# Turning a prologue block as even and odd rows in two column halves of the array, with a PSUM pair for the turns

## The chip, the cores and the metric

The kernel runs on one core of one Trainium2 chip. The metric is device time in microseconds of one execution, as the median of several runs. TensorE is called PE here (its weight loads PEld), VectorE DVE, ScalarE ACT, GpSimd POOL and SyncE SP. PE writes to PSUM, which has eight banks of 512 fp32 numbers in each of 128 partitions; ACT and DVE carry results from there to SBUF.

## The reference

Four sequences of 12544 positions and 128 channels go through a long convolution, and the result goes through a maxout feed-forward layer:

```python
h_filt = (np.maximum(pos_emb @ w1, 0.0) @ w2) * np.exp(-0.01 * pos)[:, None]
u = x * v
L = 2 * S
y = np.fft.irfft(np.fft.rfft(u, n=L, axis=1) * np.fft.rfft(h_filt, n=L, axis=0)[None], n=L, axis=1)[:, :S, :]
x = (x * y).reshape(B * S, D)                       # B=4, S=12544, D=128
h = np.maximum(np.maximum(x @ w1m, x @ w2m), x @ w3m)   # D -> 768
return h @ w_out                                    # 768 -> D
```

All of it is fp32, and the weights of the feed-forward layer come in as 64-bit numbers that the kernel converts.

## The kernel before, in words

A sequence's 12544 positions are 98 rows (`NB`) of 128. The Fourier transform is done as matrix products in two steps: a first one over the 98 rows with a table of 90 frequencies (`N1`), and a second one over the 128 positions of a row with twiddled tables. Batches 1 to 3 go through the transform beside the feed-forward layer of the batch before; batch 0 and the filter have a prologue of their own, which is what the change touches.

The schedule is written by hand: the program's order is each engine's order, and a tile framework adds the semaphores.

In the prologue the 128 channels of batch 0 are taken as 32 units (`u`) of 4 channels. For each unit, SP loads a block of `xr` and one of `vr` ([128, 4, 98], `u_load`, L381), DVE multiplies them in place (`u_mul`, L388), and PE turns the block so that the 98 rows come to lie on the partitions. `turn2(u)` (L987) turns two units at once: per unit four `nc.tensor.transpose` calls (L393), each with 98 columns of weights and the identity as the moving operand. The result is a PSUM pair (two banks, 1024 numbers in 98 partitions), which ACT copies to the tile `uT` (L993). `uT` has two buffers.

The first step is `quad` (L996), which calls `first_halves` (L172): 16 times two matmuls, in the profile 32 a quad at L178. Each takes 64 columns of `uT` as weights and 90 columns of the table `f1` as the moving operand, and goes to one half of the array's columns (PSUM partitions 0 to 63 or 64 to 127). The contraction runs over the 98 partitions. One ACT copy (L187, 128 x 720) then empties the PSUM pair. Everywhere else in the kernel the pattern is the same: two matmuls side by side in the two column halves (`halves_mm`, L169).

PSUM is four pairs, `acc[0]` to `acc[3]`, all of one name in the profile (`ps`). `turns_` hands them out. In the filter's MLP (first 38 us) it cycles over `acc[0]` and `acc[1]`, while `mlp_in` (L355, tiles of 64 rows and 41 columns) and `mlp_out` (DVE) use `acc[2]` and `acc[3]`. Afterwards it cycles over all four, in the order 2, 3, 0, 1, and turns and quads draw from the same cycle. Rows 32 to 63 of `acc[2]` and `acc[3]` are set to zero at the start (L305).

The order on PE is: warm-up matmuls; the MLP with two turns (units 0 and 1, then 2 and 3) and four early quads in between; 16 quads of the filter with two turns among them; then for each pair of units two quads and the turn of the pair after next. Loads for a pair of units are issued when a turn has freed its block six units back. Beside it DVE converts weights in small steps (`some`). After the last quad the pools are closed and the second stage begins (L1110, L169, L1135 and so on), in which `u_turn` (L395, matmul at L401) already turns blocks as even and odd rows in two column halves: `a[:, i, p::2]`, 49 columns each, to PSUM partitions 0 to 48 and 64 to 112.

Of the kernel before, what the change touches and what calls it, by code (L numbers as in the profile page):

```python
# [10 lines left out]
FP32 = mybir.dt.float32  # L11
# [5 lines left out]
P = 128  # L17
# [8 lines left out]
N1 = 90  # L26
# [5 lines left out]
def e(t):  # L32
    return np.exp(2j * np.pi * (t - np.floor(t)))


def stacked(c):

    top = np.concatenate([c.real, c.imag], -1)
    bottom = np.concatenate([-c.imag, c.real], -1)
    return np.concatenate([top, bottom], -2)  # L40


def tables(NB):
    S = P * N1
    k1 = np.arange(N1).reshape(2, N1 // 2).T.ravel()
    n = np.arange(NB)
    a = e(np.outer(n, k1 + 0.25) / N1)
    f1 = np.concatenate([a.real, a.imag], 1)
    up = e(np.outer(n + 0.5, k1 + 0.25) / N1)
    f1e = np.zeros((64 + NB // 2, 2, N1))  # L50
    for p in range(2):
        for h, t in enumerate((up, a)):
            t = t[p::2, ::2]
            f1e[64 * p:64 * p + NB // 2, h] = np.concatenate([t.real, t.imag], 1)
    f1h = np.zeros((64 + HH, 2, 2 * N1))
    f1h[:HH, 0], f1h[64:, 0] = f1[:HH], f1[HH:NH]
    f1h[:HH, 1], f1h[64:, 1] = f1[HH:NH], f1[:HH]
    f4 = np.stack([a.T.real, a.T.imag], 1) / S
    f4p = f4[::2].transpose(1, 0, 2).reshape(N1, NB // 2, 2).transpose(0, 2, 1)
    f4 = np.stack([up.T.real, up.T.imag], 1) / S  # L60
    f4s = f4[::2].transpose(1, 0, 2).reshape(N1, NB // 2, 2).transpose(0, 2, 1)
    f4q = np.stack([f4p, f4s * np.array([1, -1])[:, None]], 1)
    j, t = np.arange(64), np.arange(64)
    tw = (k1[:, None, None] + 0.25) / S
    half = []
    for r in range(2):
        s2 = (127 - 2 * t - r)[None, :, None]
        half.append(stacked(e(tw * s2 + j[None, None, :] * s2 / 128)))
    fwd = np.stack(half, 2)
    half = []  # L70
    for q in range(2):
        s2 = (2 * t + q)[None, None, :]
        half.append(stacked(e(-tw * s2 - j[None, :, None] * s2 / 128)))
    inv = np.stack(half, 2)
    both = np.stack([fwd, inv], 2)
    both = both.reshape(N1 // 2, 2, P, 2, 256).transpose(0, 2, 3, 1, 4)
    both = both.reshape(N1 // 2, P, 2, 512)
    j, t = np.arange(32), np.arange(32)
    quarter = [[], []]
    for v in range(2):  # L80
        for w in range(2):
            s2 = (63 - 2 * t - v)[None, :, None]
            quarter[0].append(stacked(e(tw * s2 + (2 * j + w)[None, None, :] * s2 / 128)))
            s2 = (2 * t + w)[None, None, :]
            quarter[1].append(stacked(e(-tw * s2 - (2 * j + v)[None, :, None] * s2 / 128)))
    quarter = np.stack([np.stack(q, 1) for q in quarter], 1)
    quarter = quarter.reshape(N1 // 2, 2, 2, 2, 2, 64, 64).transpose(0, 3, 5, 2, 1, 4, 6)
    quarter = quarter.reshape(N1 // 2, P, 2, 256)
    steps = np.zeros((N1 // 2 + LATE, P, 2, 256))
    steps[:N1 // 2, :, 0], steps[LATE:, :, 1] = quarter[:, :, 0], quarter[:, :, 1]  # L90
    f32 = np.float32
    return tuple(np.ascontiguousarray(t, f32) for t in (f1, f1e, f1h, f4q, both, steps))


@with_exitstack
def kernel(
# [15 lines left out]
    nc = tc.nc  # L112
    NG, _, _, B, NB = x.shape
# [9 lines left out]
    const = ctx.enter_context(tc.tile_pool(name="const", bufs=1))  # L123
# [8 lines left out]
    ze = dram.tile([2, 2, 2, 256], FP32, name="ze")  # L132

    f1_t, f1e_t, f1h_t, f4p_t, w_t, wq_t = tables(NB)
    f1_d = nc.inline_tensor(f1_t, name="f1_const").ap()
    f1e_d = nc.inline_tensor(f1e_t, name="f1e_const").ap()
# [4 lines left out]
    HB = NB // 2  # L141
    HR = 64 + HB
# [6 lines left out]
    w_sb = [None] + [const.tile([D, DFF], FP32, name=f"w_sb{i}") for i in (1, 2)]  # L149
    wo_sb = const.tile([P, NF, D], FP32, name="wo_sb")  # L150
    lin = const.tile([D, D], FP32, name="lin")
    f1_sb = const.tile([NB, 2 * N1], FP32, name="f1")
    f1 = f1_sb[:]
    f1e = const.tile([64 + NB // 2, 2, N1], FP32, name="f1e")
    spec = const.tile([P, N1, 2, D], FP32, name="spec")
# [8 lines left out]
    def halves_mm(out, lhsT, rhs, start, stop):  # L164


        w = block[0]
        for h in range(0, P, w):
            nc.tensor.matmul(out[h:h + w], lhsT[:, h:h + w], rhs,  # L169
                             start=start, stop=stop, skip_group_check=True)  # L170
# [95 lines left out]
    utp = ctx.enter_context(tc.tile_pool(name="utp", bufs=2))  # L266
    pro = ExitStack()
    raw0 = pro.enter_context(tc.tile_pool(name="raw0", bufs=1))
    eye = raw0.tile([P, P], FP32, name="eye")
# [5 lines left out]
    sml = fin.enter_context(tc.tile_pool(name="sml", bufs=1))  # L275
    fps = fin.enter_context(tc.tile_pool(name="fps", bufs=1, space=PSUM))
    acc = [fps.tile([P, 1024], FP32, name=f"ps{i}") for i in range(4)]
    turns_ = itertools.cycle(acc[:2])

# [17 lines left out]
    f1h = sml.tile([64 + HH, 2, 2 * N1], FP32, name="f1h")  # L299
    warm = sml.tile([P, 256], FP32, name="warm")  # L300
    nc.vector.memset(warm[:], 0.0)
    nc.vector.memset(win, 0.0)
    pms = acc[2:]
    for pm in pms:
        nc.vector.memset(pm[32:64], 0.0)  # L305
    for h in range(2):
        nc.gpsimd.dma_start(
# [14 lines left out]

    def warm_up(n):

        ps = next(turns_)
        for _ in range(n):
            halves_mm(ps[:, 0:256], warm[:, 0:P], warm[:], True, True)

    pw = next(turns_)

    def window_turn():
        nc.tensor.transpose(pw[:, 0:64 + HH], win, eye[0:64 + HH, 0:64 + HH])
# [11 lines left out]
    def w2_order():  # L344
        nc.scalar.copy(w2x[:].rearrange("f (c g) -> f c g", c=GC),
                       w2_in[:].rearrange("f (g c) -> f c g", c=GC))
# [22 lines left out]
    us, uts, ws, hts, eos, xts, xss, abs_, pss, sqs, zss = ({} for _ in range(11))  # L369
# [16 lines left out]
    def u_mul(u, eng=nc.vector):  # L386
        a, v = us[u]
        eng.tensor_tensor(out=a[:], in0=a[:], in1=v[:], op=ALU.mult)  # L388

    def turn(u, ps):  # L390
        a, _ = us.pop(u)
        for i in range(4):
            nc.tensor.transpose(ps[0:NB, i * P:(i + 1) * P], a[:, i, :], eye[:])  # L393

    def u_turn(u):  # L395
        if u % 2 == 0:
# [589 lines left out]

    def turn2(u):  # L987

        t = utp.tile([NB, 8, 2, 64], FP32, tag="uT", name="uT")
        ps = next(turns_)  # L990
        for v in range(2):
            turn(u + v, ps[:, 512 * v:512 * v + 512])
        nc.scalar.copy(t[:], ps[0:NB, :].rearrange("n (s t r) -> n s r t", s=8, r=2))  # L993
        uts[u] = t

    def quad(lhs, table, *dsts, engines=(nc.scalar.copy, nc.scalar.copy)):  # L996
# [8 lines left out]
    def early(u):  # L1005
        t, v = uts[u - u % 2], 4 * (u % 2)
        quad([t[:, v + i] for i in range(4)], (f1, f1), aside[u],
             spec[:, NS:, :, 4 * u:4 * u + 4])

    warm_up(22)  # L1010
    window_turn()
    warm_up(3)
    nc.scalar.dma_start(f1, f1_d)
    for u in range(4):
# [5 lines left out]
    for i in range(9):  # L1020
        if i in (4, 7):
            turn2(2 * (i // 7))
            for u in range(6 + 2 * (i // 7), 8 + 2 * (i // 7)):
                u_load(0, u)
        if i in (5, 6):
            early(i - 5)
        if i < 8:
            mlp_in(i)
        if i >= 7:
            early(i - 5)  # L1030
        if i == 0:
            window_back()
            nc.scalar.dma_start(f1h[:], f1h_d)
            nc.scalar.dma_start(w2_in[0:FO], w2[:, :])
            nc.scalar.dma_start(w2_in[FO:P], w2[:, :])
        else:
            mlp_out(i - 1)
        if i in (3, 5):
            for u in range(i - 3, i - 1):
                u_mul(u)  # L1040
# [1 line left out]
    for u in (0, 2):  # L1042
        uts.pop(u)
    w2_order()
    turns_ = itertools.cycle(acc[2:] + acc[:2])
    for f in range(0, FO, 4):
        quad([hs[:, f + i] for i in range(4)], (f1h[:, 0], f1h[:, 1]), specH[:, :, :, f:f + 4])
        u, k = divmod(f // 4, 4)
        if u < 2:
            if k in (0, 1):  # L1050
                u_mul(2 * u + 4 + k)
            if k == 2:
                turn2(2 * u + 4)
                for v in range(2 * u + 10, 2 * u + 12):
                    u_load(0, v)
        some(2 if u < 2 and k < 2 else 3)
# [3 lines left out]
    for u in range(4, NU, 2):  # L1060
        t = uts.pop(u)
        for v in range(2):
            if u + 4 < NU:
                u_mul(u + 4 + v)
            at = 4 * (u + v)
            dst = spec[:, :, :, at:at + 4]
            quad([t[:, 4 * v + i] for i in range(4)], (f1, f1),
                 *([dst] if u + v < NU - 1 else [dst[:, :NK], dst[:, NK:]]),
                 engines=copies if u + v == NU - 1 else copies[:1])
            some(1)  # L1070
        if u + 4 < NU:
            turn2(u + 4)
        for v in (u + 10, u + 11):
            if v < NU:
                u_load(0, v)
        if u in (22, 24, 26):
            wf[(u - 22) // 2] = load_dir((u - 22) // 2, 0)
            wi[(u - 22) // 2] = load_dir((u - 22) // 2, 1)
        some(2)
# [261 lines left out]
    for i in range(0, NT, 2):  # L1341
        h = {}
        X, Y = banks if i % 4 == 0 else banks[::-1]
        for j, (name, f) in enumerate(ORDER):
            n = int(name[1]) - 1
# [66 lines left out]
```

## Time and profile before

| | us |
|---|---|
| median of three runs | 2207.23 (2205.39 to 2209.17) |
| the profiled execution | 2205.64 |
| its span | 2203.9 |
| PE busy | 2186.5 (99%) |
| turns of the prologue (L393) | 128 matmuls, 24.1 to 104 |
| prologue's last quad | ends at 109.3 |
| second stage's first matmul (L1110) | 110.41 |

The page's first lines give the busy time of each engine and its share of the span. A line of the order of time has a start, a length, the engine, the line of the kernel, the operation, the tiles written and read, the array's tile (rows by columns), the moving operand's shape and a count. The length of a group reaches to the end of its last matmul, which overlaps the next group; the pace is therefore read from start to start. A table of stretches has a row for each stretch with the busy time of each engine (with the number of instructions), PE's granted clock as a share of full speed, and the DMA's share and rate.

### The profile page before, as it was taken

To read this page: it belongs to the slowest core of one execution; us is meant where nothing else is said; L and a number is where in the kernel's file an instruction comes from. 1 tells how busy PE (TensorE), PEld (TensorE's weight loads), DVE (VectorE), ACT (ScalarE), POOL (GpSimd) and SP (SyncE) were. 2 spreads that over 40 slices of the span, in tenths; PEclk is the share of its full clock that TensorE was granted. 3 is DMA by queue.
4 is the path that set the end of the run, shared out by engine and by line. 5 is a ranking of instruction groups with operands and counts; after the bars stand their busy time and mean duration, and the time that the engine had idled before them with its cause. 6 is when DMAs were issued, how large, how long until landed. Compare 5 with 4: busy or idle time off the path is not lost.

```text
span 2203.9 us, 77207 instructions
## 1 busy us (share of the span) xinstructions
PE 2186.5 (99%) x31655; PEld 1258.5 (57%) x31655; DVE 1533.7 (70%) x3292; ACT 1211.4 (55%) x2223; POOL 1183.3 (54%) x1580
## 2 busy tenths in 40 slices
PE   9999999999999999999999999999999999999998
PEld 8988855555555555555555455555555545555565
DVE  5688966678888766668888766668878745454443
ACT  3699845466666555466666555456666522222222
POOL 1166568545544667535455566534545326666665
PEclk9999999999999999999999999999999999999999
DMA  8789999879999899789999899879999622222221
GB/s 200 184 262 318 302 181 206 170 196 247 248 245 246 209 189 178 155 193 243 245 245 251 212 193 175 171 172 244 242 251 241 179 75 59 65 71 69 59 59 24
DMA packets 491270, 411.62 MB, mean 187 GB/s; under 512 B 289379, under 2 KB 407901, under 8 KB 490917
## 3 DMA queue, kind: packets, MB, share of 16 engines
q1 hardware_dynamic: 443495, 274.33, 57.5%
q0 software_dynamic: 45936, 130.43, 20.9%
q8 instruction: 249, 4.08, 0.8%
q10 hardware_dynamic: 1486, 1.93, 0.4%
q14 instruction: 104, 0.85, 0.1%
HBM read 262.85 MB, written 84.68 MB: 158 GB/s over the span
## 4 chain that ended last, share of the span: by engine, by line
PE 93%; DVE 2%; POOL 2%; issue 1%; DMA 0%; ACT 0%; POOLq 0%; ACTq 0%; DVEq 0%
PE hps L169 46%; PE ops L169 20%; PE ops L913 6%; PE cps L169 4%; PE cps L549 3%; PE cps L451 3%; PE ps L178 3%; PE cps L559 3%; PE ps L169 2%; POOL xt L640 1%; PE last L169 1%; DVE ab L647 1%; PE ps L393 1%; DVE xs L639 1%; POOL specH L640 1%
## 5 line engine op out<-in xcount | busy, mean ns | idle before, releaser
L169 PE MATMUL hps<-gt,w_sb 128*64 128x392 f32 (+1 forms) x7672 | 1151.8, 494 | 1.8 <-DVE hid L852 1.0
L849 ACT ACTIVATE hid<-hps 128x392 f32<-128x392 f32 x768 | 382.4, 498 | 745.2 <-PE hps L169 726.9
L169 PEld LDWEIGHTS hps<-gt,w_sb 128*64 128x64 f32 (+1 forms) x7672 | 413.7, 126 | 454.5 <-issue 415.9
L852 DVE TENSOR_TENSOR hid<-hid,hps 128x392 f32<-128x392 f32 x768 | 428.5, 558 | 339.9 <-PE hps L169 321.4
L169 PE MATMUL ops<-hid,wo_sb 128*64 128x392 f32 x2304 | 476.8, 492 | 0.0
L601 POOL TENSOR_TENSOR cb<-cb,xs 128x512 f32<-128x512 f32 x135 | 178.2, 1320 | 358.3 <-DVE xs L598 349.8
L169 PEld LDWEIGHTS ops<-hid,wo_sb 128*64 128x64 f32 x2304 | 165.7, 137 | 213.5 <-issue 213.5
L574 DVE TENSOR_TENSOR cb<-cps,eo 128x512 f32<-128x512 f32 (+1 forms) x288 | 175.2, 650 | 78.0 <-ACT eo L571 76.9
L867 POOL DMA_DIRECT2D out_dram<-ot x96 | 77.1, 803 | 263.6 <-ACT ot L865 247.3
L589 ACT ACTIVATE xs<-cb 32x512 f32<-32x512 f32 x270 | 169.5, 628 | 21.9 <-DVE cb L574 13.1
L590 ACT COPY xs<-cb 32x512 f32<-32x512 f32 x270 | 166.3, 616 | 3.1
L605 DVE TENSOR_TENSOR xs<-cb 128x256 f32<-128x256 f32 x270 | 148.3, 598 | 7.3 <-POOL cb L601 7.3
L431 ACT COPY uT<-turned 113x512 uint16<-113x512 uint16 x180 | 125.9, 770 | 1.9 <-DMA turned<-planes 1.7
L388 POOL TENSOR_TENSOR ut<-ut 128x392 f32<-128x392 f32 x90 | 92.8, 1032 | 43.1 <-DMA ut<-in_vr_dram 42.9
L582 POOL DMA_DIRECT2D zd<-cb x135 | 93.8, 695 | 39.9 <-DVE cb L574 36.8
L169 PEld LDWEIGHTS cps<-f4p,even 90*64 90x64 f32 x1552 | 87.2, 138 | 35.9 <-issue 33.1
L777 POOL DMA_DIRECT2D xT<-in_x_dram x172 | 101.4, 605 | 4.6 <-DVE ab L647 3.1
L473 DVE TENSOR_TENSOR low<-high,cps 128x180 f32<-128x180 f32 x186 | 54.7, 336 | 68.9 <-ACT high L463 68.9
L938 POOL DMA_DIRECT2D out_dram<-o x120 | 72.6, 610 | 45.6 <-DVE o L931 44.5
L169 PE MATMUL cps<-f4p,zt 90*64 90x49 f32 x1552 | 95.9, 222 | 0.0
L415 POOL COPY planes<-ut 128x392 uint16<-128x392 uint16 x180 | 94.9, 561 | 0.0
L169 PE MATMUL cps<-f4p,even 90*64 90x49 f32 x1552 | 94.6, 220 | 0.0
(173 smaller groups left out, 3306.1 us busy)
## 6 DMA issues: line engine op xcount, KB each, us to landing
ht<-hd SPq DMA_DIRECT2D x264, 256.0 KB, 6.8
wt<-wq_const POOLq DMA_DIRECT2D x144, 256.0 KB, 5.6
zd<-cb POOLq DMA_DIRECT2D x135, 256.0 KB, 5.1
zt<-zd SPq DMA_DIRECT2D x384, 90.0 KB, 3.8
sq<-spec SPq DMA_DIRECT2D x528, 64.0 KB, 5.9
ut<-in_xr_dram SPq DMA_DIRECT2D x128, 196.0 KB, 4.0
ut<-in_vr_dram SPq DMA_DIRECT2D x128, 196.0 KB, 4.3
wt<-wt_const SPq DMA_DIRECT2D x90, 256.0 KB, 5.1
```

Source lines behind the costliest of these rows:

```text
L169: nc.tensor.matmul(out[h:h + w], lhsT[:, h:h + w], rhs, start=start, stop=stop, skip_group_check=True)
L415: nc.gpsimd.tensor_copy(w[:, h, :, :, 0:HB], a[:].bitcast(U16).rearrange("p s (m e h) -> p h s e m", e=2, h=2)[:, h])
L431: nc.scalar.copy(uts[u][0:HR, 8 * (u % 2):8 * (u % 2) + 8].rearrange("n s r t -> n (s r t)").bitcast(U16).rearrange("n (s r t h) -> n h s ...
L574: nc.vector.tensor_tensor(out=cb[:, a, lo:hi], in0=ps[:, lo:hi], in1=eo[:, lo:hi], op=op)
L589: nc.scalar.mul(xs[at:at + 32], xt[at + 32:at + 64], -1.0)
L590: nc.scalar.copy(xs[at + 32:at + 64], xt[at:at + 32])
L601: nc.gpsimd.tensor_tensor(out=xts[g], in0=xts[g], in1=xs[:], op=ALU.add)
L605: nc.vector.tensor_tensor(out=ab[:, q], in0=y[:, 0], in1=y[:, 1], op=(ALU.subtract, ALU.add)[q])
L777: eng.dma_start(xT[c * NG:(c + 1) * NG].rearrange("d i p n -> d (i p) n"), x[:, 4 * i:4 * i + 8, c, b, :])
L849: nc.scalar.activation(h[:], pa[:, 0:N], Relu)
L852: nc.vector.tensor_tensor(out=h[:], in0=h[:], in1=pb[:, 0:N], op=ALU.max)
L913: nc.tensor.matmul(ps[32 * q:32 * q + 32, 0:H2], w[:, m:m + 32], rhs[:, H2 * c:H2 * c + H2], start=start, stop=True, skip_group_check=True)
```

## The change

`turn2` no longer calls `turn` (which goes away) but multiplies the even rows and the odd rows of the block with the identity, as two matmuls of 49 columns in the two column halves. `uT` then has the even rows in partitions 0 to 48 and the odd ones in 64 to 112, and nothing in between. The table `f1` is laid out to match: `f1x` has 113 rows, with zeros in rows 49 to 63. The turns always use `acc[1]`, whose rows 32 to 63 are set to zero at the start. The quads use `acc[0]`, `acc[0]`, `acc[0]`, `acc[2]` in the MLP part and then cycle over `acc[0]`, `acc[3]`, `acc[2]`. The warm-up goes to `acc[0]`. Here `HB` is 49 and `HR` 113.

```diff
+    f1x = np.zeros((64 + NB // 2, 2 * N1))
+    f1x[:NB // 2], f1x[64:] = f1[::2], f1[1::2]
...
-    return tuple(np.ascontiguousarray(t, f32) for t in (f1, f1e, f1h, f4q, both, steps))
+    return tuple(np.ascontiguousarray(t, f32) for t in (f1x, f1e, f1h, f4q, both, steps))
...
-    f1_sb = const.tile([NB, 2 * N1], FP32, name="f1")
+    f1_sb = const.tile([HR, 2 * N1], FP32, name="f1")
...
-    turns_ = itertools.cycle(acc[:2])
+    turns_ = iter((acc[0], acc[0], acc[0], acc[2]))
...
-    for pm in pms:
+    for pm in acc[1:]:
         nc.vector.memset(pm[32:64], 0.0)
...
-        ps = next(turns_)
         for _ in range(n):
-            halves_mm(ps[:, 0:256], warm[:, 0:P], warm[:], True, True)
-
-    pw = next(turns_)
+            halves_mm(acc[0][:, 0:256], warm[:, 0:P], warm[:], True, True)
+
+    pw = acc[0]
...
-    def turn(u, ps):
-        a, _ = us.pop(u)
-        for i in range(4):
-            nc.tensor.transpose(ps[0:NB, i * P:(i + 1) * P], a[:, i, :], eye[:])
...
-        t = utp.tile([NB, 8, 2, 64], FP32, tag="uT", name="uT")
-        ps = next(turns_)
+        t = utp.tile([HR, 8, 2, 64], FP32, tag="uT", name="uT")
+        ps = acc[1]
         for v in range(2):
-            turn(u + v, ps[:, 512 * v:512 * v + 512])
-        nc.scalar.copy(t[:], ps[0:NB, :].rearrange("n (s t r) -> n s r t", s=8, r=2))
+            a, _ = us.pop(u + v)
+            for i in range(4):
+                for p in range(2):
+                    nc.tensor.matmul(
+                        ps[64 * p:64 * p + HB, 512 * v + i * P:512 * v + (i + 1) * P],
+                        a[:, i, p::2], eye[:], start=(i == 0), stop=True,
+                        skip_group_check=True)
+        nc.scalar.copy(t[:], ps[0:HR, :].rearrange("n (s t r) -> n s r t", s=8, r=2))
...
-    turns_ = itertools.cycle(acc[2:] + acc[:2])
+    turns_ = itertools.cycle((acc[0], acc[3], acc[2]))
```

## The prediction

> **What bounds the kernel now.** I read the page first (busy shares), then a table of busy time for the stretches of the prologue, then the PE's order of time in that stretch, and last the DVE's, to see what feeds the turns. The page:
>
> ```profile
> span 2203.9 us, 77207 instructions
> PE 2186.5 (99%) x31655; PEld 1258.5 (57%) x31655; DVE 1533.7 (70%) x3292; ACT 1211.4 (55%) x2223; POOL 1183.3 (54%) x1580
> ```
>
> The PE is busy for 99% of the span, so a microsecond of PE work taken out is a microsecond of time unless another engine then holds the PE up. The turns all lie between 24 and 104 us. One stretch of the table from one turn's start to the next, and one of the PE in order of time (start, length, line, names, count):
>
> ```profile
> core 0: us, PE busy (x) PEld busy (x) DVE busy (x) ACT busy (x) POOL busy (x), PEclk, DMA share, GB/s
> 66.68:70.32 3.64, 3.64 (x75) 3.35 (x73) 1.03 (x2) 2.53 (x3) 0.00 (x0) 1.00 1.18 296
> ...
> 88.52:92.17 3.65, 3.65 (x75) 3.36 (x73) 3.29 (x8) 2.54 (x3) 0.00 (x0) 1.00 0.92 218
> ```
>
> ```profile
> 31.27 1.87 PE L355 MATMUL ps<-w_sb,specH 64*41 64x64 f32 x64
> 33.06 1.08 PE L393 MATMUL ps<-eye,ut 128*98 128x128 f32 x8
> 34.08 1.75 PE L355 MATMUL ps<-w_sb,specH 64*41 64x64 f32 x64
> 35.75 2.70 PE L178 MATMUL ps<-f,uT 98*64 98x90 f32 x64
> ...
> 43.12 5.18 PE L178 MATMUL ps<-f1h,spec 105*64 105x90 f32 x128
> 48.23 1.08 PE L393 MATMUL ps<-eye,ut 128*98 128x128 f32 x8
> 49.24 11.38 PE L178 MATMUL ps<-f1h,spec 105*64 105x90 f32 x288
> 60.45 2.65 PE L178 MATMUL ps<-f,uT 98*64 98x90 f32 x64
> 63.04 1.08 PE L393 MATMUL ps<-eye,ut 128*98 128x128 f32 x8
> 64.05 2.70 PE L178 MATMUL ps<-f,uT 98*64 98x90 f32 x64
> 66.68 1.08 PE L393 MATMUL ps<-eye,ut 128*98 128x128 f32 x8
> ```
>
> The reader is to see that the PE never pauses here at full clock, that ACT has over a microsecond to spare in 3.64, and that a cycle is one turn (1.01 from its start to the next group's) and two quads (64 matmuls, 2.63). The same half-array turn that the change brings already runs later, in `u_turn`, again between other matmuls of the PE:
>
> ```profile
> 236.88 1.09 PE L169 MATMUL ps<-ab,wt 128*64 128x128 f32 x16
> 237.81 1.04 PE L401 MATMUL pst<-eye,ut 128*49 128x128 f32 x16
> 238.68 0.61 PE L1110 MATMUL gps<-wt,specH 128*64 128x128 f32 x8
> 239.12 1.04 PE L169 MATMUL ps<-spec,wt 128*64 128x128 f32 x16
> ```
>
> **The change part by part.** Sums are made against the profiled execution: 2205.64 us, of which 2203.9 is the span. It lies 1.59 under the median of the three runs (2207.23), and I add that back at the end.
>
> *Turns.* Removed: 8 full-array transposes per `turn2`, 1.01 us (64.05 - 63.04), so 127 ns each. Added: 16 matmuls of 49 columns by 128. L401 runs exactly this form, 16 in 0.87 us (238.68 - 237.81), 54.4 ns each. Saved 0.14 us. The 16 weight loads (8 before) take 124 ns each in both forms, but in L401 they lie under the other half's matmuls, or the pace couldn't be 54.4.
>
> *The bubble ahead of a turn.* From 43.12 to 48.23 are 128 quad matmuls and one change to a turn, 5.11 us; from 49.24 to 63.04 are 352 and one change, 13.80. The difference is 8.69 for 224, 38.8 ns each. 64 of them take 2.48, yet between turns they take 2.63: 0.15 us go each time the PE passes from halves to the full array. Around L401 I see none: 16 in 0.87 before L1110, which then runs 8 in 0.44, the same 54 ns. After the change turn and quad both use the full rows in two column halves, as L169 and L401 do. The cost of the new passage isn't in the trace: between nothing (L401) and 0.15 (L393 now). I take nothing, as the nearest row; the other end stays for the range. The Trainium skill, "TensorEngine Tiling (Array Packing)", Key Properties, says that a change of tiling mode, though not of the tile, drains the TensorE. By that rule the bubble goes with the mode change, and the trace's 0.15 beside L393 and 0 beside L401 agree; the sum by the rule would be the one I take.
>
> So a turn among quads saves 0.14 + 0.15 = 0.29 us, and a cycle goes from 3.64 to 0.87 + 2.48 = 3.35. There are 14 such turns (2 among the filter's quads, 12 among the units'): 4.0 us.
>
> *The two turns among the filter MLP* (L355, tiles of 64 rows). There the change of mode stays: 32 quad matmuls between L355s (26.80 to 28.20) take 1.40 against 32 x 38.8 = 1.24, a bubble of 0.16. Now the bubble there is 0.12 (1.79 for 64 of L355 ahead of the turn at 33.06, 1.67 without). So each saves 0.14 + 0.12 - 0.16 = 0.10: 0.2 us.
>
> *Quads with 113 rows in place of 98.* The pace does not follow the rows: 98 rows and 105 rows both go at 38.8 (the run from 49.24 holds both). Nothing.
>
> *PSUM.* The turns get a pair of their own, and quads rotate over three instead of all over four. A quad's copy on ACT begins 0.1 after its last matmul and takes 0.76; its pair comes up again two quads (2.48) later, so some 1.6 us are left over. A turn's copy (1.01) now has a cycle of 3.35 less the turn itself, 2.48. On ACT a copy of a turn and two of quads are 2.53 in 3.35: it keeps up. In the early part two quads share one pair in succession: the first's copies end at 29.14, the second starts at 29.87. The tightest is the first filter quad, now on the pair of the third early quad: copies end at 38.09, it starts at 38.28. Both move together; I put it at nothing, and at most 0.1.
>
> *Other edits.* One more DVE memset of 0.91 us at 3.7 us: DVE then stands idle up to 18.65. The table grows from 98 to 113 rows on ACT's DMA queue, issued at 13.6 and first used at 26.8; 15 more rows of 720 bytes cover no part of that. The copy of a turn reads 113 partitions by 1024 in place of 98 by 1024, one ACT instruction as before. SP's and POOL's queues issue what they did, in the same order. A turn waits for one more product no earlier than before, since the order of units is unchanged.
>
> *What feeds the turns.* A turn needs the DVE product of two blocks, which needs their loads. The tight stretch:
>
> ```profile
> 85.37 0.57 DVE L388 TENSOR_TENSOR ut<-ut 128x392 f32<-128x392 f32 x1 [1.57 <-DMA ut<-in_vr_dram]
> ...
> 88.52 0.57 DVE L388 TENSOR_TENSOR ut<-ut 128x392 f32<-128x392 f32 x1 [0.66 <-DMA ut<-in_vr_dram]
> ```
>
> The DVE waits for loads, but ahead of the PE: the product that ends at 85.94 is the second block of the turn at 88.52. After the change this turn starts 0.2 + 9 x 0.29 = 2.8 earlier, at 85.7, and reaches its second block 0.4 later, at 86.1. So even if no load came sooner, the product would be there by 0.2. The other turns have as much or more (the last: 99.32 against 99.1 + 0.4). And loads will come sooner, since the SP issues them when a turn frees its block.
>
> *Sum.* 4.0 + 0.2 = 4.2 us, all on the chain: the last quad ends 4.2 sooner, and the next stage (first matmul at 110.41, after the last quad's copies) starts by as much sooner. 2205.6 - 4.2 = 2201.4; beside the median 2207.2 - 4.2 = 2203.0.
>
> **The rivals.**
>
> *The bubble stays.* If quads of 113 rows and turns of 128 still cost 0.15 at each passage, a turn saves 0.14: 14 x 0.14 + 0.2 = 2.2, 2205.0. For it: the bubble is seen between the very groups at hand; against: none beside L401.
>
> *The PE waits for products.* If the DMA is at its limit (shares of 0.9 to 1.3 in the table) and contention makes loads later than now, the cycle stays at 3.64 from the turn at 73.96 on, and only 5 turns and the first 0.2 gain: 1.6 us, 2205.6. Against: the 0.2 us or more worked out above, with loads no sooner than today.
>
> *Slower: the weight loads come into the open.* If in this place the 16 loads of 124 ns were not under the matmuls, a turn would take 16 x 0.124 = 1.98 against 1.16 now with its bubble, and 14 x 0.82 + 2 x 1.0 = 13.5 us come on: 2220.7. It breaks even at 72 ns a matmul and is 0.2% slower from 90. For it: L393's 127 ns is just about its load's 124; against: L401 at 54.4 with the same loads and the same strided block.
>
> *Slower: the plain product is the dear form.* If the transposes are quick only because they are transposes, and the same work as a multiplication costs four times 127 ns a block, 8 x 0.51 = 4.1 a turn adds 16 x 3.0 = 48 us: 2255. The Trainium skill, "TensorE: Matmul & The Clock Gate", Terms, has transpose mode as four times faster for FP32, and the tiling page says that column tiling shuts it off for FP32 input. Against it: L401 is that plain product in column halves, and does a block in 0.44.
>
> **How the numbers follow.** Forecast 80%, bubble stays 7%, PE waits 6%, weight loads 5%, dear product 2%. About 0.2% (4.4 us) is what a measurement here can tell from no change. The forecast lies at -0.19%, just short of it; its runs spread by some 2 us to either side (2205.39 to 2209.17 before), so its 80% part into 44 faster and 36 same. The next two are same. Faster 0.44, same 0.49, slower 0.07. The range reaches from 2203.0 by that spread and some more below, 2199.5, and over the cases at 2205.0 and 2205.6 with their spread, 2207.5; the slower cases stay out.
>
> **What the profile after would show.** The turn as a group of 256 matmuls of 128x49 at 16 in 0.87; turns 3.35 us apart; the second stage's first matmul at about 106.2; PE without a pause up to there. Wrong if the stretch from turn to turn stays near 3.5 (bubble), if the PE's idle time names a DVE product or an ACT copy, or if a matmul of the new turn takes above 72 ns. A prologue shorter by 4.2 with a total that isn't would mean that the later stages took it back.

## The result and the profile after

The changed kernel takes 2217.05 us (median of six runs) against 2207.61 for the kernel before, a ratio of 1.0043 with a 95% interval of 1.0033 to 1.0053: slower by 7.3 to 11.7 us. The forecast was 2203.0, faster by 4.2.

The page of the changed kernel, span and busy time:

```profile
span 2214.9 us, 77975 instructions
PE 2197.3 (99%) x32039; PEld 1306.8 (59%) x32039; DVE 1534.1 (69%) x3293; ACT 1211.0 (55%) x2223; POOL 1183.0 (53%) x1580
```

PE is busy for 10.8 us more (2197.3 against 2186.5) and has 384 matmul records more (32039 against 31655), while its idle time (17.6 us against 17.4) and the busy times of DVE, ACT and POOL are much as they were. The PE in order of time (start, length, line, names, count), at the places that the prediction showed:

```profile
32.09 0.73 PE L356 MATMUL ps<-w_sb,specH 64*41 64x64 f32 x18
33.18 1.30 PE L356 MATMUL ps<-w_sb,specH 64*41 64x64 f32 x46 [0.36 <-issue]
34.41 1.96 PE L991 MATMUL ps<-eye,ut 128*49 128x128 f32 x32
36.30 1.75 PE L356 MATMUL ps<-w_sb,specH 64*41 64x64 f32 x64
...
52.70 11.36 PE L180 MATMUL ps<-f1h,spec 105*64 105x90 f32 x288
63.86 2.68 PE L180 MATMUL ps<-f,uT 113*64 113x90 f32 x64
66.34 1.95 PE L991 MATMUL ps<-eye,ut 128*49 128x128 f32 x32
68.09 2.69 PE L180 MATMUL ps<-f,uT 113*64 113x90 f32 x64
70.57 1.95 PE L991 MATMUL ps<-eye,ut 128*49 128x128 f32 x32
...
120.91 0.66 PE L1112 MATMUL gps<-wt,specH 128*64 128x128 f32 x8 [1.11 <-DVE spec L189]
```

A turn has 32 records, not the 16 that the forecast counted, and takes 1.75 us (68.09 - 66.34) instead of 1.01. From turn to turn it is 4.23 us, where it was 3.64. The second stage starts at 120.91 instead of 110.41, 10.5 us later. What follows it takes 2094.0 us of the span against 2093.5: the later stages neither added nor gave back more than half a microsecond.

The reason for the 32 shows when records are counted against calls, and it could have been seen before. A call is one matmul or transpose as the code issues it; a record is one entry of the profile. A row for each of three lines of the code of the kernel before has the number of records after the x (then the shortest, median and longest in ns, the first and last start):

```profile
L393 PE MATMUL ps<-eye,ut x128: 272/273/318, 24.1 to 103.9; 128*98 128x128 f32 x128
...
L178 PE MATMUL ps<-f,uT x1024: 238/241/293, 26.8 to 109.0; 98*64 98x90 f32 x171
...
L401 PE MATMUL pst<-eye,ut x64: 272/273/273, 233.6 to 257.2; 128*49 128x128 f32 x64
```

and the turn's line of the changed kernel:

```profile
L991 PE MATMUL ps<-eye,ut x512: 270/272/317, 24.1 to 114.6; 128*49 128x128 f32 x171
```

Sixteen turns of 8 transposes are 128 calls, and there are 128 records: one each. The 32 unit quads have 16 calls each, 512, and 1024 records. The turns on L401 shown here are 4 calls of `u_turn` with 8 matmuls, 32, and there are 64 records. The changed kernel's 16 turns are 256 matmul calls, and there are 512. So in these rows a plain fp32 matmul leaves two records, a transpose one. (The account of `quad` above, "16 times two matmuls", is the same misreading: the code has 16 matmuls, which leave 32 records.)

### The profile page after: what moved, and what is told of

The parts are those of the page before. It is cut to its first block, busy times and chain, and to the rows that moved or that the text cites. A ratio compares the mean times of both kernels' runs of the same rounds, so it can differ in the third digit from the quotient of the medians.

```text
span 2214.9 us, 77975 instructions
## 1 busy us (share of the span) xinstructions
PE 2197.3 (99%) x32039; PEld 1306.8 (59%) x32039; DVE 1534.1 (69%) x3293; ACT 1211.0 (55%) x2223; POOL 1183.0 (53%) x1580
## 4 chain that ended last, share of the span: by engine, by line
PE 93%; DVE 2%; POOL 2%; issue 1%; ACT 0%; DMA 0%; POOLq 0%; SPq 0%; DVEq 0%; ACTq 0%
PE hps L171 46%; PE ops L171 20%; PE ops L909 6%; PE cps L171 4%; PE cps L545 3%; PE cps L447 3%; PE ps L180 3%; PE cps L555 3%; PE ps L171 2%; PE ps L991 1%; POOL xt L636 1%; PE last L171 1%; DVE ab L643 1%; DVE xs L635 1%; PE ps L356 1%
## 5 line engine op out<-in xcount | busy, mean ns | idle before, releaser
L171 PEld LDWEIGHTS hps<-gt,w_sb 128*64 128x64 f32 (+1 forms) x7672 | 430.6, 126 | 439.3 <-issue 406.6
```

Of the source, the lines that this page charges most:

```text
L171: nc.tensor.matmul(out[h:h + w], lhsT[:, h:h + w], rhs, start=start, stop=stop, skip_group_check=True)
```

## The experiments

Each kernel was timed beside the kernel before on the same chip, and the rows stand in the order of the sections below; "second stage" is the start of its first matmul, "cycle" the time from one turn to the next among the units, and "turn" is the cycle less two quads (64 records at 38.8 ns, 2.48 us), so with all its passages.

| kernel | median us (that of before) | ratio, 95% | second stage | cycle | turn |
|---|---|---|---|---|---|
| before | | | 110.41 | 3.64 | 1.16 |
| changed | 2217.05 (2207.61) | 1.0043, 1.0033 to 1.0053 | 120.91 | 4.23 | 1.75 |
| pair only | 2208.2 (2207.41) | 1.0001, 0.9991 to 1.0010 | 111.33 | 3.64 | 1.16 |
| halves, shared pairs | 2219.54 (2207.41) | 1.0056, 1.0041 to 1.0071 | 123.97 | 4.23 | 1.75 |
| plain, full array | 2222.09 (2207.41) | 1.0066, 1.0051 to 1.0081 | 124.67 | 4.55 | 2.07 |
| turns twice | 2221.80 (2207.41) | 1.0065, 1.0050 to 1.0080 | 124.53 | 4.51 | 2.03 |
| one pass | 2201.24 (2207.99) | 0.9971, 0.9961 to 0.9982 | 104.88 | 2.94 | 0.46 |
| late only | 2216.33 (2207.99) | 1.0032, 1.0020 to 1.0045 | 119.86 | 4.23 | 1.75 |

### The PSUM part alone

```diff
-    turns_ = itertools.cycle(acc[:2])
+    turns_ = iter((acc[0], acc[0], acc[0], acc[2]))
...
-        ps = next(turns_)
+        ps = acc[1]
         for v in range(2):
             turn(u + v, ps[:, 512 * v:512 * v + 512])
...
-    turns_ = itertools.cycle(acc[2:] + acc[:2])
+    turns_ = itertools.cycle((acc[0], acc[3], acc[2]))
```

> The kernel before with the PSUM part of the change alone: turns as full-array transposes, but in a pair of their own, quads over the three others, one more memset. Theory A (the new turn is dearer because each plain fp32 product shows as two matmul records, where a transpose shows as one; PSUM plays no part): as before, 2207.6 within 0.1%, turn to turn 3.64 us, second stage's first matmul at 110.4 us. Theory B (turns and quads wait for the copies, since a quad's pair comes up again after three and the turns have one pair): most of the 9.4 us is here, about 2217, with PE waits on ACT named.

The time is that of before, and so is the cycle. The PE's waits from 36 us to the second stage (line waiting, releaser, total, times, longest), the whole answer:

```profile
engine line waited for: us in total, times, longest us
PE gps L1109 <- DVE spec L187: 1.1, 1, 1.1
```

No quad and no turn waits for a copy: three pairs for the quads and one for the turns are enough, as worked out before the run. Theory B falls. The 0.9 us by which the second stage starts later lie in the MLP, where the PE pauses (0.47 us in one place) and some of its groups take longer; more on that at the end.

### The new turn in the old PSUM order

```diff
-    turns_ = iter((acc[0], acc[0], acc[0], acc[2]))
+    turns_ = itertools.cycle(acc[:2])
...
-    for pm in acc[1:]:
+    for pm in acc:
         nc.vector.memset(pm[32:64], 0.0)
...
-        ps = acc[1]
+        ps = next(turns_)
...
-    turns_ = itertools.cycle((acc[0], acc[3], acc[2]))
+    turns_ = itertools.cycle(acc[2:] + acc[:2])
```

> The changed kernel with the PSUM order of before: half-array turns, but turns and quads draw from one cycle over all four pairs (rows 32 to 63 of all four are zeroed at the start, the gap rows then hold old quad values that meet zeros in the table). Theory A: as the changed kernel, 2217 within 0.1%, 32 records a turn in 1.75 us, turn to turn 4.23, second stage at 120.9. Theory B: back to about 2207.6.

The cycle is the changed kernel's 4.23, as the first records of two turns in a row show (single records of neighbouring groups change places in this order, so a turn's first record can stand alone):

```profile
69.29 0.27 PE L992 MATMUL ps<-eye,ut 128*49 128x128 f32 x1
...
73.52 0.28 PE L992 MATMUL ps<-eye,ut 128*49 128x128 f32 x1
```

The total is 0.3 us above the band that was expected, and the second stage starts 3.1 us later than in the changed kernel. Of this, 2.3 us are there at the first turn (26.37 against 24.07), for a reason of the experiment's own: the warm-up matmuls now go to pairs that the DVE first sets to zero, and the PE waits for it:

```profile
PE ps L171 <- DVE ps L307: 3.6, 1, 3.6
```

By that the MLP starts at 18.42 instead of 15.84. From the first turn to the second stage it takes 97.60 us, in the changed kernel 96.84 (120.91 - 24.07), before 86.30 (110.41 - 24.11). Over half of the 0.8 us between the first two lies in the MLP again, and no run told its cause. The new turn carries the loss, whichever pairs it writes.

### A plain product on the full array

```diff
-            nc.tensor.transpose(ps[0:NB, i * P:(i + 1) * P], a[:, i, :], eye[:])
+            nc.tensor.matmul(ps[0:NB, i * P:(i + 1) * P], a[:, i, :], eye[:],
+                             start=(i == 0), stop=True, skip_group_check=True)
```

> The kernel before with each transpose of the prologue's turns replaced by a plain matmul with the identity, on the full array, nothing else changed. Theory A: two records for each of the 128 products; if a record of 128 columns holds the whole array as long as a pair of half-array records holds it (107 ns) a turn takes 1.71 us, if its weight load sets the pace (127 ns) 2.03; so 16 turns add 11 to 16 us, 2219 to 2224, as much as the changed kernel or more. Rival C (going to column halves is what costs, plain or not): as before, 2207.6.

Nothing but the kind of matmul differs from the kernel before, and the cycle is longer than the changed kernel's, 4.55 us against 4.23 (the intervals of the two totals overlap slightly):

```profile
66.40 1.99 PE L393 MATMUL ps<-eye,ut 128*98 128x128 f32 x16
68.31 2.70 PE L178 MATMUL ps<-f,uT 98*64 98x90 f32 x64
70.95 1.99 PE L393 MATMUL ps<-eye,ut 128*98 128x128 f32 x16
```

Now there are 16 records for 8 calls. Rival C, that the column halves are the dear part, falls: giving up the transpose is what costs, and the halves win some of it back (turn 1.75 against 2.07).

### Every turn twice

```diff
         for v in range(2):
+            for i in range(4):
+                nc.tensor.transpose(ps[0:NB, 512 * v + i * P:512 * v + (i + 1) * P],
+                                    us[u + v][0][:, i, :], eye[:])
+        for v in range(2):
             turn(u + v, ps[:, 512 * v:512 * v + 512])
```

> The kernel before with every turn's 8 transposes issued twice, the second time over the first: PE work doubled, result the same. If the prologue's PE time is wholly exposed: 16 x 1.01 = 16.2 us more, 2223.8, second stage at 126.6. If loads or DVE products have cover to give: clearly less than 16.

```profile
66.67 1.08 PE L993 MATMUL ps<-eye,ut 128*98 128x128 f32 x8
67.58 1.04 PE L393 MATMUL ps<-eye,ut 128*98 128x128 f32 x8
68.55 2.70 PE L178 MATMUL ps<-f,uT 98*64 98x90 f32 x64
71.18 1.08 PE L993 MATMUL ps<-eye,ut 128*98 128x128 f32 x8
```

The second stage starts 14.1 us later than before, and the total is 11.0 to 17.7 us longer. From the first turn on it is 13.85 us, and 16 times the 0.87 of a cycle would be 13.9: the added PE time is fully exposed. The expected 16.2 was too much because eight more transposes cost 0.87 us (4.51 - 3.64), not the 1.01 between a turn's start and the next quad's. So of the 1.16 that a turn costs before, 0.87 are transposes, and the 0.29 left over are put down to the two passages, into the full array and out of it. The forecast had seen only the first, 0.15; the other was inside the 1.01.

### One pass

```diff
+    eyeh = sml.tile([P, P], mybir.dt.bfloat16, name="eyeh")
...
+    nc.vector.tensor_copy(eyeh[:], eye[:])
...
-                        a[:, i, p::2], eye[:], start=(i == 0), stop=True,
-                        skip_group_check=True)
+                        a[:].bitcast(mybir.dt.bfloat16)[:, i, 2 * p + 1::4], eyeh[:],
+                        start=(i == 0), stop=True, skip_group_check=True)
```

> The changed kernel with the turn's operands read as bf16: the upper halves of the block's fp32 numbers as weights and a bf16 identity, same 16 products a turn, same halves, same PSUM pair. It leaves out the lower 16 bits of the turned block. Theory A (the second record is the price of fp32 in a plain product): one record a product, 16 a turn at 54 ns, 0.87 us, turn to turn 3.35 us, second stage at about 106.3, total 4.2 us under before, 2203.4: the forecast's sum. Rival D (the number of PE instructions, or the passage between turns and quads, costs): stays above before.

The total is under that of before by 4.0 to 8.6 us. One record a call, as theory A has it, but shorter than it said. The row of the turn's matmuls, and the first records of two turns in a row:

```profile
L993 PE MATMUL ps<-eyeh,ut x256: 217/219/265, 24.4 to 98.6; 128*49 128x128 bf16 x128
...
62.70 0.22 PE L993 MATMUL ps<-eyeh,ut 128*49 128x128 bf16 x1
...
65.64 0.22 PE L993 MATMUL ps<-eyeh,ut 128*49 128x128 bf16 x1
```

The cycle is 2.94 us (65.64 - 62.70), so a turn is 0.46, 29 ns a record, where 54 was expected: a record of fp32 takes almost twice as long as one of bf16 of the same shape. With 256 matmul calls in this kernel and in the changed one alike, the number of calls and the passages between turns and quads cost nothing that could make up the loss: rival D falls. From the turn at 80.3 on, the PE begins to wait for what feeds it:

```profile
PE ps L993 <- DVE ut L391: 2.2, 3, 1.0
```

These are the DVE products, which wait for loads. At that turn the PE is 4.6 us ahead of the kernel before (80.29 against 84.88). Up to there the loads kept pace; the forecast needed 2.5 us at that turn. From the first turn to the second stage 5.8 us are gained (80.49 against 86.30), where the 16 shorter turns by themselves would give some 10.6 (14 x 0.70 and 2 x 0.42): the rest goes to these waits, 2.2, to longer turns around them, and to pauses and longer groups in the MLP.

### The first two turns as before

```diff
+            if u < 4:
+                for i in range(4):
+                    nc.tensor.transpose(ps[0:NB, 512 * v + i * P:512 * v + (i + 1) * P],
+                                        a[:, i, :], eye[:])
+                continue
...
-        quad([t[:, v + i] for i in range(4)], (f1, f1), aside[u],
+        quad([t[:, v + i] for i in range(4)], (f1o, f1o), aside[u],
```

> The changed kernel with the first two turns, those among the filter's MLP, as full-array transposes again (with the old table beside the new one for their four early quads). Theory A: each of the two gives back 1.89 - 1.01 = 0.88 us, and the PE's pause of 0.36 us in the MLP that the changed kernel shows may go too: 1.8 to 2.2 us under the changed kernel, about 2215, second stage at 118.8 to 119.1, PE cycle later still 4.23.

By the total this can't be told from the changed kernel (the intervals overlap). In the trace, from the first turn to the second stage it takes 95.26 us (119.86 - 24.60), 1.6 less than the changed kernel's 96.84. The two turns give back 0.88 each, 1.76 in all, and the PE's pause in this stretch did not go but was longer, 0.57 instead of 0.36:

```profile
38.26 1.32 PE L182 MATMUL ps<-f1o,uT 98*64 98x90 f32 x29 [0.57 <-issue]
```

The second stage starts later than expected (119.86) because the first turn, too, starts 0.5 us later. The size of the two turns is right; that the pause hung on them is not borne out.

## Why the prediction was wrong

**The step that failed** is the price of the new turn: "Added: 16 matmuls of 49 columns by 128. L401 runs exactly this form, 16 in 0.87 us". The form was right and the unit wrong. `turn2` calls 16 matmuls, for two units. L401's 16 are records, of 8 calls, for one unit. The right reading of that row is 2 x 0.87 = 1.74 us a turn, and 1.75 was measured. The forecast's own sign of being wrong, a matmul of the new turn above 72 ns, came true: 1.75 us for 16 calls is 109 ns. The 16 weight loads and the group of 256 matmuls that it names are 32 and 512 records for the same reason. The kernel before had all that was needed: x128 on L393 for 128 calls, and x1024 on L178 for 512.

**The sum with that term mended.** A turn among quads then costs 1.75 - 1.01 = 0.74 more and saves the 0.15 bubble: 0.59 by 14, 8.3 us. The two turns in the MLP cost 0.88 more each (1.89 against 1.01), 1.8. With the pause of 0.36 this makes 10.4; the trace has 96.84 - 86.30 = 10.5 from the first turn to the second stage.

**What held.** The prologue is bound by PE, and what a turn loses there goes into the total: turns twice, +14.1 us at the second stage. What a turn gains goes there only until the PE comes to wait for the products, as with one pass. The bubble goes when turn and quad share the column halves: in the changed kernel 352 quad records from 52.70 to 66.34 take 13.64 us where 13.80 were before. It was undersized: 0.29 in all by the turns done twice, of which 0.14 stood in the sum as part of the turn. The quads of 113 rows keep their pace (2.48 for 64), and the PSUM order costs nothing that the totals show. The changed kernel's turns waited for no product, but they came later than before and so are no test; the test is the one-pass kernel, whose first such wait, 0.48 us, came with the PE 4.6 us ahead.

**The rivals.** The plain product as the dear form was the right one, at 2%. It was put aside with the same wrong reading ("does a block in 0.44": 8 of L401's records are half a block). Its price was too high, 4.1 us a turn against 1.75, and two things make the difference. A plain product on the full array costs 1.78 us for 8 calls (2.07 less 0.29, if the passages cost it what they cost the transposes), twice the transposes' 0.87, not four times. And the halves spare the 0.29. The Trainium skill, "TensorE: Matmul & The Clock Gate", Terms, gives transpose mode as four times faster for FP32; here it is 2.0 times. Had I followed that rule instead of my reading of the row, the sign would have been right, though not the size. The rival of weight loads in the open didn't come: 512 loads of 125 ns a piece run at one in 55 ns. The bf16 ones of the one-pass kernel are as long, 123 ns, and run at one in 29, so the length of a load's record isn't what sets the pace. What within the PE sets it, no run told apart.

**What was not tried.** Fewer passages with the transposes kept, by grouping turns two by two, would spare at most 7 x 0.29 = 2.0 us, under 0.1%, by an estimate from the rows above. It would also ask for half of the products two quads (2.48 us) earlier or free half of the buffers that much later, and before the products had only 2.7 us to spare at the turn at 73.96 and 2.6 at 88.52. None of the kernels that compute the whole result beats the one before.

## What to carry to other kernels

Before a duration is carried from one line to another, divide its records by the calls in the code: a count in the profile is of records, and one plain fp32 matmul left two here. The fp32 transposes of this kernel were worth keeping as transposes: a plain product with the identity took twice their time (1.78 us against 0.87), and packing it in column halves gave back little more than the passages (2.07 to 1.75). A written rule that speaks against a change deserves a second look at the row that seems to refute it.

## What the runs showed of the hardware

- Time of one call with 128 moving columns, from the turn column: a full-array fp32 transpose 109 ns (0.87 us for 8), a plain full-array fp32 product 223 ns (1.78 for 8), a plain fp32 product on half the columns 109 ns (1.75 for 16), a bf16 one on half the columns 29 ns (0.46 for 16). So plain fp32 costs 3.8 times bf16 on half the columns. The Trainium skill, "FP8 and Floating Point Precision", TensorE Precision Notes, says that true FP32 takes four passes through the array; the 3.8 here is near that, and the trace shows two records a call, without telling which passes a record holds.
- A passage from column halves to the full array and back costs 0.29 us in all beside the quads of this kernel, 0.15 of it ahead of the full-array group and 0.14 behind it.
- In the MLP part the PE pauses for a few tenths of a microsecond, where the profile names only "issue". Ahead of the first turn all kernels have such a pause. Between the first turn and the second stage the kernel before has none, the changed one 0.36 us, the pair alone 0.47, the halves in shared pairs 0.29, one pass 1.1 in three places, late only 0.57 (in the quads just behind the MLP), the plain full-array turns and the doubled ones none. No run told the cause, and it is below what the totals can tell.
